# Where TensorE's operand tiles begin in SBUF: a fused attention and feed-forward kernel on one core

## The chip, the core and the metric

The kernel runs on one core of a Trainium2 chip. The metric is the device time of one execution in microseconds. The page and the trace are of one execution, taken by the hardware profiler.

## What is computed

For 4 batches, 8 heads, 576 positions and a head width of 64, two attentions are added: one over positions averaged by fours (each of its rows then stands for four positions), and one over a band of 7 positions. The sum, 2304 rows of 512, goes through two feed-forward layers.

```python
out_up = np.repeat(sm_attn(q_d, k_d, v_d), factor, axis=2)   # q_d: means of 4 positions
mask = np.abs(pos[:, None] - pos[None, :]) < factor          # factor = 4
out_local = softmax(where(mask, scale * q @ k.T, -1e9)) @ v
x = (out_up + out_local) as (2304, 512)
g = x @ w_gate                                               # 512 -> 1536
x = (g * sigmoid(g) * (x @ w_val)) @ w_out                   # 1536 -> 512
h = x @ w_in                                                 # 512 -> 2048
out = (h * clip(h + 3, 0, 6) / 6) @ w2_out                   # 2048 -> 512
```

## The kernel before, in words

Rows of x are worked on in five blocks of 512, 384, 512, 512 and 384 rows (`BLOCKS`, in units of 64). For each block a list of units is gone through: a unit is one 128-wide piece of a weight matrix. The kinds are G (gate), V (value), O (first output), H (second input) and P (second output). G and V of a block come first, with O two pieces behind, then H, with P two behind; this order of `units` and the look-ahead of `prefetch` set the order of nearly everything else. Attention for the next block is cut into small steps between the units (`down_main`, `chunk_scores`, `unit_values`, `step_x`).

Products are made in three parts of type float32r: each operand is kept as a high part, rounded by ScalarE, and a low part, the remainder, subtracted by VectorE. `split_unit` does it for a weight piece (`wr`, L230 and L231, out of the float32 weights `w32`, tag `wst`), `put_cols` for x (`xr`, L265 and L266), `run_unit` for the middle products (`g`, L965 and L966), `put_x2` for the first layer's result (`x2`, L1003 and L1004). TensorE then multiplies high by high, low by high and high by low.

`run_unit` has the two matmul lines. L948 serves G, V and H: the stationary operand is a 128 x 128 piece of `wr`, the moving one 512 or 384 columns of `xr` (G, V: the trace's pG, pV) or of `x2` (H: pH), into two PSUM banks in turn. L990 serves O and P: for O (aO) the stationary operand is `wr` and `g` moves; for P (aP) a 128 x 128 piece of `g` is stationary and 512 columns of `wr` move. Every such matmul has its own weight load.

Weights come from HBM once, as 8-byte words in block 0 (tag `w64`), are decoded on ScalarE and VectorE (`decode_a` L210, `decode_b` L219), and stored as float32 to `kept`, from which the later blocks load them (`load_unit` L178). The small constants are `half1` (0.5, a bias), `ones_last` (a mask of 28 numbers for either edge) and what those are made from (`ih`, `ind`). `softmax_d` keeps the negated maxima (`nm`) and the sums (`sd`) of the coarse attention. Before the first gate unit, matmuls on the bf16 tile `idle` fill TensorE (L94, L435).

SBUF tiles of a pool lie one behind the other, in the order in which their tags first appear, each on a multiple of 32 bytes of its partition. In the built program the tiles that matter begin at these bytes (modulo 256 in brackets), each further buffer of a tag one tile on:

| tile (tag) | bytes of one buffer | buffers | first byte |
|---|---|---|---|
| sl | 2048 | 3 | 21,536 (32) |
| x2 | 16,384 | 1 | 27,680 (32) |
| g | 4096 | 4 | 44,064 (32) |
| w64 | 4104, 4128 apart | 4 | 60,448 (32) |
| xr | 16,384 | 2 | 76,960 (160) |
| w32 (wst) | 4096 | 3 | 126,624 (160) |
| wr | 4096 | 4 | 138,912 (160) |

All slices of these that TensorE reads begin a multiple of 512 bytes into them, but for the first gate piece of block 0, which is done in 244 and 268 columns.

Of the kernel before, what the change touches and what calls it, by code (L numbers as in the profile page):

```python
# [10 lines left out]
F32 = mybir.dt.float32  # L11
# [3 lines left out]
I16 = mybir.dt.int16  # L15
# [6 lines left out]
P = 128  # L22
# [15 lines left out]
EXP_AT = 26  # L38

EARLY = 6  # L40


@with_exitstack
def tile_kernel(
# [14 lines left out]
    B, H, S, D = q.shape  # L59
    DM = H * D  # L60
# [4 lines left out]
    NJH = NJ // 2  # L65
    W = 7
# [3 lines left out]
    UT = 4 * NSEG  # L70
# [4 lines left out]
    UMAX = max(BLOCKS)  # L75
# [5 lines left out]
    cp = ctx.enter_context(tc.tile_pool(name="cp", bufs=1))  # L81
    sp = ctx.enter_context(tc.tile_pool(name="sp", bufs=2))
# [12 lines left out]

    ident = cp.tile([P, P], F32, name="ident")
    make_identity(nc, ident)
    half1 = cp.tile([P, 1], F32, name="half1")
    nc.gpsimd.memset(half1, 0.5)

    ones_last = []
    for side in range(2):
        ih = cp.tile([P, H], F32, tag=f"ih{side}", name=f"ih{side}")
        nc.gpsimd.memset(ih, 0.0)
        nc.gpsimd.affine_select(
            out=ih, in_=ih, compare_op=ALU.not_equal, fill=NEG,
            base=-(NSEG - 1) * side, pattern=[[-NSEG, H]], channel_multiplier=1,
        )
        ind = cp.tile([P, 1], F32, tag=f"ind{side}", name=f"ind{side}")
        nc.vector.tensor_reduce(ind, ih, axis=AX.X, op=ALU.add)  # L110
        on = cp.tile([P, 4, W], F32, tag=f"on{side}", name=f"on{side}")
        nc.gpsimd.memset(on, 0.0)
        sgn = 1 if side == 0 else -1
        nc.gpsimd.affine_select(
            out=on, in_=on, compare_op=ALU.is_ge, fill=1.0,
            base=-3 if side == 0 else 6, pattern=[[sgn, 4], [sgn, W]], channel_multiplier=0,
        )
        nc.vector.tensor_scalar(on, on, ind[:, 0:1], None, op0=ALU.mult)
        ones_last.append(on)
# [10 lines left out]
    def behind(ins):  # L130

        if front[0]:
            tc.keep_in_program_order(ins)
# [22 lines left out]
    raw = {}  # L156
# [3 lines left out]
    def view(t, i):  # L160
        return t[:, i % 2, :].rearrange("p (c e) -> p c e", c=NC)

    def load_raw(i):
        if units[i][2] == 0:
            load_unit(i)

    def load_kept(i):
        if units[i][2]:
            load_unit(i)

    def load_unit(i):
        kind, f, bi = units[i]
        if bi or not wide:
            if i % 2 == 0:
                w32[i // 2] = sp.tile([P, 2, DM], F32, tag="wst", name=f"w32_{i}", bufs=3)
        if bi:
            if i % 2 == 0:
                nc.sync.dma_start(w32[i // 2], kept[i % NU // 2])  # L178
            return
        src = wsrc[kind]  # L180
        if wide:
            src = src.bitcast(I16)
        m = 4 if wide else 1
        if kind in "GVH":
            src = src[:, f * P * m:(f + 1) * P * m].rearrange("(c p) f -> p c f", p=P)
        else:
            src = src[f * P:(f + 1) * P, :].rearrange("p (c e) -> p c e", c=NC)
        if wide:
            raw[i] = sp.tile([P, 4 * DM + 4], I16, tag="w64", name=f"w64_{i}", bufs=4)
            behind(nc.sync.dma_start(raw[i][:, 1:1 + 4 * DM].rearrange("p (c e) -> p c e", c=NC), src))  # L190
        else:
            nc.sync.dma_start(view(w32[i // 2], i), src)
# [500 lines left out]


    def softmax_d(pool, ps, nm_, bufs):
        nm = pool.tile([NJH, 2], F32, tag="nm", name=f"nm{nm_}", bufs=8)
        nc.vector.tensor_reduce(nm, ps, axis=AX.X, op=ALU.max, negate=True)
        pd = pool.tile([NJH, 2, NJ], F32, tag="pd", name=f"pd{nm_}", bufs=bufs)
        sd = pool.tile([NJH, 2], F32, tag="sd", name=f"sd{nm_}", bufs=8)
        for half in range(2):  # L700
            nc.scalar.activation(
                pd[:, half], ps[:, half], AF.Exp, bias=nm[:, half:half + 1], accum_out=sd[:, half:half + 1]
            )
        return pd, sd
# [155 lines left out]
    def down_main(b, dn, qk):  # L860
# [3 lines left out]
        def score(c):  # L864

            pss = []
            for par in range(2):
                ps = bank(("pa", "px")[par], f"pS{b}_{2 * c + par}")[:NJH, :2 * NJ]
                pss.append(ps.rearrange("p (g j) -> p g j", g=2))
            for half in range(2):  # L870
                for par in range(2):
                    rows = slice(par * D, par * D + D)
                    tc.keep_in_program_order(nc.tensor.matmul(  # L873
                        pss[par][:, half], qk["q"][rows, c, half * NJH:(half + 1) * NJH], qk["k"][rows, c, :],
                        start=True, stop=True,
                    ))

            def use():
                for par in range(2):
                    h = 2 * c + par  # L880
                    st[h] = softmax_d(ap, pss[par], f"{b}_{h}", 4)
                defer(1, lambda: [norm_d(*st[2 * c + par]) for par in range(2)])

            return use
# [154 lines left out]
    def load_ahead(n):  # L1039
        nonlocal loaded  # L1040
        while loaded < min(n, len(chunks)):
            load_chunk(*chunks[loaded])
            loaded += 1

    for bi in range(NB):
# [37 lines left out]
        for i in range(bi * NU, (bi + 1) * NU):  # L1083
# [21 lines left out]
            next(main, None)  # L1105
            if m == NU - EARLY:
                load_ahead(at + 1)
# [40 lines left out]
```

## Time and profile before

| | us |
|---|---|
| median of 3 runs (lowest, highest) | 1000.89 (1000.48, 1002.2) |
| span of the profiled execution | 998.5 |
| the median over this span | 2.4 |
| TensorE (PE) busy | 956.0 |
| VectorE (DVE) busy | 773.1 |
| ScalarE (ACT) busy | 529.7 |
| GpSimd (POOL) busy | 114.5 |

The span is the profiled execution's own time from its first to its last instruction; the runs' times hold what lies around it as well, so the profiled execution counts as 998.5 + 2.4 = 1000.9 us. Its mean granted TensorE clock was 0.978 of 2.4 GHz. A matmul's busy time in the groups overlaps with the next one's; the time from one matmul to the next is read from the chain or the timeline. PEld is the weight load, which runs beside PE.

### The profile page before, as it was taken

What the parts mean: (1) busy time and instruction counts of PE and PEld (TensorE: products, weight loads), DVE (VectorE), ACT (ScalarE), POOL (GpSimd) and SP (SyncE); (2) the same over time, 40 slices, a digit from 0 to 9 for tenths busy, and PEclk for the clock granted to TensorE, in tenths of its full rate; (3) what the DMA queues carried; (4) which work ended last, traced back from release to release, by engine and by line L of the source; (5) the groups of instructions that cost most, each with busy time, mean ns of one, the idle gap of its engine ahead of it and who ended that gap; (6) DMA issues with size and microseconds to landing.
All of it is one profiled execution on the core that took longest, in us unless ns stands there. A gap on an engine that the chain in (4) does not pass through costs nothing.

```text
span 998.5 us, 13508 instructions
## 1 busy us (share of the span) xinstructions
PE 956.0 (96%) x4797; PEld 797.6 (80%) x4800; DVE 773.1 (77%) x1237; ACT 529.7 (53%) x1115; POOL 114.5 (11%) x113
## 2 busy tenths in 40 slices
PE   8769999999998999996999999999999999999997
PEld 4558888777897987875888777788888888999996
DVE  6597986799989989996984699998346995545653
ACT  4566566876543577552334764453335444544553
POOL 5590000000046000004620000000000000000000
PEclk9769999999999999997999999999999999999999
DMA  9979899466789322356553122363322233533331
GB/s 191 201 197 344 292 331 324 144 217 231 250 244 289 117 85 87 118 177 205 159 172 106 58 70 96 104 228 121 102 88 89 83 104 109 154 125 124 125 126 52
DMA packets 83655, 160.72 MB, mean 161 GB/s; under 512 B 19460, under 2 KB 51716, under 8 KB 83588
## 3 DMA queue, kind: packets, MB, share of 16 engines
q1 hardware_dynamic: 78692, 142.03, 45.6%
q10 hardware_dynamic: 4896, 17.83, 5.1%
q8 instruction: 38, 0.62, 0.3%
q14 instruction: 29, 0.24, 0.1%
HBM read 137.29 MB, written 22.54 MB: 160 GB/s over the span
## 4 chain that ended last, share of the span: by engine, by line
PE 72%; issue 14%; DVE 4%; DMA 4%; POOL 3%; SPq 2%; ACT 0%; POOLq 0%; ACTq 0%; DVEq 0%
PE pH L948 16%; PE aP L990 16%; PE aO L990 13%; PE pG L948 13%; PE pV L948 12%; SPq L126 2%; DMA nq<-in_q_dram 1%; DVE wr L231 1%; POOL nq L290 1%; DMA w<-kept 1%; DMA vd<-in_v_dram 1%; PE pS L873 1%; PE pO L723 1%; DMA w<-in_moe_w_val_dram 1%; DMA nv<-in_v_dram 0%
## 5 line engine op out<-in xcount | busy, mean ns | idle before, releaser
L231 DVE TENSOR_TENSOR wr<-w,wr 128x512 fp32r<-128x512 f32 x340 | 238.3, 705 | 119.1 <-ACT wr L230 117.6
L230 ACT ACTIVATE wr<-w 128x512 fp32r<-128x512 f32 x340 | 212.0, 627 | 175.3 <-PE pV L948 53.9
L990 PE MATMUL aP<-wr,gH 128*128 128x512 f32 x864 | 216.3, 399 | 0.7 <-ACT wr L230 0.4
L948 PE MATMUL pH<-x,wr 128*128 128x512 f32 (+1 forms) x960 | 216.0, 376 | 0.0
L948 PEld LDWEIGHTS pH<-x,wr 128*128 128x128 f32 x960 | 173.6, 188 | 28.0 <-issue 2.7
L990 PEld LDWEIGHTS aP<-wr,gH 128*128 128x128 f32 x864 | 159.8, 188 | 39.0 <-issue 2.5
L948 PE MATMUL pG<-xr,wr 128*128 128x512 f32 (+3 forms) x732 | 161.3, 375 | 5.1 <-ACT xr L265 4.4
L948 PE MATMUL pV<-xr,wr 128*128 128x512 f32 (+1 forms) x720 | 156.1, 372 | 5.3 <-DVE wr L231 4.1
L990 PE MATMUL aO<-gV,wr 128*128 128x512 f32 (+1 forms) x720 | 156.3, 373 | 0.3 <-DVE wr L231 0.3
L948 PEld LDWEIGHTS pG<-xr,wr 128*128 128x128 f32 x732 | 136.2, 195 | 24.0 <-ACT xr L265 5.0
L948 PEld LDWEIGHTS pV<-xr,wr 128*128 128x128 f32 x720 | 132.7, 190 | 23.5 <-DVE wr L231 4.8
L990 PEld LDWEIGHTS aO<-gV,wr 128*128 128x128 f32 x720 | 131.6, 188 | 19.7 <-DVE wr L231 0.6
L963 ACT ACTIVATE h<-pH,half 128x512 f32<-128x512 f32 (+1 forms) x80 | 51.5, 644 | 71.4 <-PE pH L948 71.2
L954 ACT ACTIVATE sl<-pG 128x512 f32<-128x512 f32 (+1 forms) x60 | 33.2, 554 | 72.1 <-PE pG L948 70.5
L964 DVE SCALAR_TENSOR_TENSOR h<-h,pH 128x512 f32<-128x512 f32 (+1 forms) x80 | 50.5, 631 | 25.0 <-ACT h L963 24.2
L210 ACT ACTIVATE top<-w 128x512 f16<-128x512 bf16 x68 | 52.9, 790 | 15.6 <-DVE w L219 6.8
L782 DVE TENSOR_TENSOR pr<-q,k 128x1792 f32<-128x1792 f32 x27 | 57.0, 2113 | 3.9 <-DMA k<-in_k_dram 3.8
L290 POOL TENSOR_TENSOR nq<-nq 72x512 f32<-72x512 f32 x12 | 18.9, 1572 | 347.4 <-DMA nq<-in_q_dram 347.4
L965 ACT ACTIVATE gH<-h 128x512 fp32r<-128x512 f32 (+1 forms) x80 | 46.9, 587 | 19.1 <-DVE h L964 17.1
L966 DVE TENSOR_TENSOR gH<-h,gH 128x512 fp32r<-128x512 f32 (+1 forms) x80 | 50.6, 634 | 5.8 <-ACT gH L965 4.8
L819 DVE TENSOR_TENSOR pv<-sc,v 128x1792 f32<-128x1792 f32 x27 | 54.5, 2020 | 0.3
L965 ACT ACTIVATE gV<-sl 128x512 fp32r<-128x512 f32 (+1 forms) x60 | 35.2, 586 | 36.3 <-DVE sl L960 35.5
(127 smaller groups left out, 809.2 us busy)
## 6 DMA issues: line engine op xcount, KB each, us to landing
w<-kept SPq DMA_DIRECT2D x136, 512.0 KB
kept<-w ACTq DMA_DIRECT2D x34, 512.0 KB
w<-in_moe_w_out_dram SPq DMA_DIRECT2D x28, 512.0 KB
w<-in_moe_w_in_dram SPq DMA_DIRECT2D x16, 512.0 KB
w<-in_moe_w_gate_dram SPq DMA_DIRECT2D x12, 512.0 KB
w<-in_moe_w_val_dram SPq DMA_DIRECT2D x12, 512.0 KB
out_dram<-os SPq DMA_DIRECT2D x16, 256.0 KB
nq<-in_q_dram SPq DMA_DIRECT2D x12, 288.0 KB
```

Of the source, the lines that this page charges most:

```text
L210: behind(nc.scalar.activation(halves(top[i % 2], 2, F16)[:, :, 1], h3.bitcast(BF16), AF.Copy))
L230: behind(nc.scalar.activation(r[:, 0], s, AF.Copy))
L231: behind(nc.vector.tensor_tensor(r[:, 1], s, r[:, 0].bitcast(F32), op=ALU.subtract))
L782: nc.vector.tensor_tensor(pr, qt[:, a:a + SUB, None, :].to_broadcast([P, SUB, W, D]), win(kt, a, SUB), op=ALU.mult)
L819: nc.vector.tensor_tensor(pr, pe[:, a:a + SUB, :, None].to_broadcast([P, SUB, W, D]), win(vt, a, SUB), op=ALU.mult)
L948: nc.tensor.matmul(ps[:, cs], r[:, a, c], x[:, c, b_, cs], start=part is HIGH and a == c == 0, stop=part is LOW and c == NC - 1,)
L954: nc.scalar.activation(sl, ps, AF.Silu)
L963: nc.scalar.activation(h, ps, AF.Relu, scale=1 / 6, bias=half1[:, 0:1])
L964: nc.vector.scalar_tensor_tensor(h, h, 1.0, ps, op0=ALU.min, op1=ALU.mult)
L965: nc.scalar.activation(g[:, 0, :nt], h, AF.Copy)
L966: nc.vector.tensor_tensor(g[:, 1, :nt], h, g[:, 0, :nt].bitcast(F32), op=ALU.subtract)
L990: nc.tensor.matmul(ps, **one, start=f_ == 0 and a == b_ == 0, stop=f_ == nf - 1 and b_ == 1,)
```

## The change

The small constants (`half1` and the two masks) share one tile of 384 bytes, `consts`; `ih` and `ind` become slices of a buffer of the tag `sl`; `nm` and `sd` share one tile; and `w64` is 4160 bytes instead of 4104. The tiles behind them move by at most 96 bytes:

| tile (tag) | first byte before (modulo 256) | after |
|---|---|---|
| sl | 21,536 (32) | 21,504 (0) |
| x2 | 27,680 (32) | 27,648 (0) |
| g | 44,064 (32) | 44,032 (0) |
| w64 | 60,448 (32) | 60,416 (0), further buffers at 64, 128, 192 |
| xr | 76,960 (160) | 77,056 (0) |
| w32 (wst) | 126,624 (160) | 126,720 (0) |
| wr | 138,912 (160) | 139,008 (0) |

The buffers of each but `w64` all have the remainder of the first. Every engine's instructions and its waits on semaphores stand in the same order in both built programs, SyncE's DMAs too; only names and addresses differ. The changed kernel's lines lie 2 to 4 lines lower in the file.

```diff
@@ -38,6 +38,8 @@
 EXP_AT = 26
 
 EARLY = 6
+
+SMALL = 384
 
 
 @with_exitstack
@@ -95,20 +97,22 @@
 
     ident = cp.tile([P, P], F32, name="ident")
     make_identity(nc, ident)
-    half1 = cp.tile([P, 1], F32, name="half1")
+    consts = cp.tile([P, SMALL // 4], F32, name="consts")
+    half1 = consts[:, 56:57]
     nc.gpsimd.memset(half1, 0.5)
 
     ones_last = []
     for side in range(2):
-        ih = cp.tile([P, H], F32, tag=f"ih{side}", name=f"ih{side}")
+        tmp = sp.tile([P, UMAX * UT], F32, tag="sl", name=f"tmp{side}", bufs=3)
+        ih = tmp[:, :H]
         nc.gpsimd.memset(ih, 0.0)
         nc.gpsimd.affine_select(
             out=ih, in_=ih, compare_op=ALU.not_equal, fill=NEG,
             base=-(NSEG - 1) * side, pattern=[[-NSEG, H]], channel_multiplier=1,
         )
-        ind = cp.tile([P, 1], F32, tag=f"ind{side}", name=f"ind{side}")
+        ind = tmp[:, H:H + 1]
         nc.vector.tensor_reduce(ind, ih, axis=AX.X, op=ALU.add)
-        on = cp.tile([P, 4, W], F32, tag=f"on{side}", name=f"on{side}")
+        on = consts[:, 28 * side:28 * side + 28].rearrange("p (t w) -> p t w", w=W)
         nc.gpsimd.memset(on, 0.0)
         sgn = 1 if side == 0 else -1
         nc.gpsimd.affine_select(
@@ -186,7 +190,7 @@
         else:
             src = src[f * P:(f + 1) * P, :].rearrange("p (c e) -> p c e", c=NC)
         if wide:
-            raw[i] = sp.tile([P, 4 * DM + 4], I16, tag="w64", name=f"w64_{i}", bufs=4)
+            raw[i] = sp.tile([P, 4 * DM + 32], I16, tag="w64", name=f"w64_{i}", bufs=4)
             behind(nc.sync.dma_start(raw[i][:, 1:1 + 4 * DM].rearrange("p (c e) -> p c e", c=NC), src))
         else:
             nc.sync.dma_start(view(w32[i // 2], i), src)
@@ -693,10 +697,10 @@
 
 
     def softmax_d(pool, ps, nm_, bufs):
-        nm = pool.tile([NJH, 2], F32, tag="nm", name=f"nm{nm_}", bufs=8)
+        ns = pool.tile([NJH, 2, 2], F32, tag="ns", name=f"ns{nm_}", bufs=8)
+        nm, sd = ns[:, 0], ns[:, 1]
         nc.vector.tensor_reduce(nm, ps, axis=AX.X, op=ALU.max, negate=True)
         pd = pool.tile([NJH, 2, NJ], F32, tag="pd", name=f"pd{nm_}", bufs=bufs)
-        sd = pool.tile([NJH, 2], F32, tag="sd", name=f"sd{nm_}", bufs=8)
         for half in range(2):
             nc.scalar.activation(
                 pd[:, half], ps[:, half], AF.Exp, bias=nm[:, half:half + 1], accum_out=sd[:, half:half + 1]
```

## Rows read from the trace of the kernel before

**Rows 1.** The page: busy us of each engine, share of the span, instructions.

```profile
PE 956.0 (96%) x4797; PEld 797.6 (80%) x4800; DVE 773.1 (77%) x1237; ACT 529.7 (53%) x1115; POOL 114.5 (11%) x113
```

**Rows 2.** Windows by stage: stretch and its length, busy of each engine, clock, DMA share.

```profile
75.00:168.00 93.00, 93.00 (x413) 76.35 (x413) 77.35 (x107) 59.46 (x97) 0.00 (x0) 0.99 0.94 327
168.00:275.00 107.00, 106.69 (x517) 82.67 (x516) 96.09 (x175) 77.22 (x167) 0.00 (x0) 1.00 0.63 215
275.00:335.00 60.00, 54.46 (x298) 52.87 (x297) 55.18 (x61) 24.57 (x45) 30.76 (x24) 0.97 0.77 233
335.00:400.00 65.00, 63.44 (x378) 54.62 (x377) 59.19 (x125) 46.25 (x121) 0.00 (x0) 1.00 0.31 100
400.00:467.00 67.00, 58.20 (x285) 48.61 (x285) 62.57 (x98) 31.88 (x60) 8.39 (x6) 0.97 0.48 149
...
553.00:656.00 103.00, 102.91 (x496) 78.68 (x495) 92.06 (x177) 59.40 (x140) 0.00 (x0) 1.00 0.28 93
656.00:756.00 100.00, 100.00 (x438) 81.95 (x437) 64.13 (x78) 39.94 (x67) 0.00 (x0) 1.00 0.38 127
```

**Rows 3.** Waits of PE: total us, times, longest.

```profile
PE pqT L303 <- POOL dnq L291: 8.1, 2, 5.4
...
PE pV L948 <- DVE wr L231: 4.1, 2, 3.5
```

**Rows 4.** Groups of PE by shape: form xcount | busy us, mean ns.

```profile
L990 PE MATMUL aP<-wr,gH 128*128 128x512 f32 x864 | 216.3, 399 | 0.7 <-ACT wr L230 0.4 <-DVE wr L231 0.3
L948 PE MATMUL pH<-x,wr 128*128 128x512 f32 x576 | 143.8, 399 | 0.0
L990 PE MATMUL aO<-gV,wr 128*128 128x512 f32 x432 | 103.3, 395 | 0.0
L948 PE MATMUL pG<-xr,wr 128*128 128x512 f32 x420 | 102.2, 399 | 0.4 <-ACT xr L265 0.4
L948 PE MATMUL pV<-xr,wr 128*128 128x512 f32 x432 | 101.4, 390 | 0.0
L948 PE MATMUL pH<-x,wr 128*128 128x384 f32 x384 | 72.3, 340 | 0.0
L948 PE MATMUL pV<-xr,wr 128*128 128x384 f32 x288 | 54.8, 344 | 5.3 <-DVE wr L231 4.1 <-ACT sl L954 1.1
L990 PE MATMUL aO<-gV,wr 128*128 128x384 f32 x288 | 53.0, 339 | 0.3 <-DVE wr L231 0.3
L948 PE MATMUL pG<-xr,wr 128*128 128x384 f32 x288 | 52.0, 335 | 0.0
```

**Rows 5.** The chain that ended last: start us, us to the next piece, work.

```profile
709.00 5.44 PE pV L948 x24
714.45 5.59 PE aO L990 x24
...
798.57 5.59 PE pH L948 x24
804.16 5.57 PE aP L990 x24
...
853.67 4.16 PE pV L948 x24
...
866.15 4.22 PE aO L990 x24
...
937.41 4.22 PE pH L948 x24
```

**Rows 6.** Timeline of PE, bf16 filler matmuls: start us, us, instruction.

```profile
6.21 0.59 PE L435 MATMUL fTq<-idle 128*128 128x512 bf16 x2
6.64 0.25 PE L446 MATMUL fTq<-ident,fnq 96*128 96x96 f32 x1
```

**Rows 7.** Groups by shape, of DVE: form xcount | busy us, mean ns | idle before.

```profile
L231 DVE TENSOR_TENSOR wr<-w,wr 128x512 fp32r<-128x512 f32 x340 | 238.3, 705 | 119.1 <-ACT wr L230 117.6
...
L966 DVE TENSOR_TENSOR gH<-h,gH 128x512 fp32r<-128x512 f32 x48 | 32.9, 686 | 4.1 <-ACT gH L965 3.3
```

## The prediction

> **What bounds the kernel now.** I read the page's first part first, then the stretches by stage, then what PE waits for, then the counts of matmuls by shape, and last the chain of work that ended last, which gives the time from one matmul to the next. TensorE (PE) is busy 956.0 us of the 998.5 us span, 96% [rows 1]. By stages it is full: in the gate/value/out stage of block 0 (75 to 168 us) 93.00 of 93.00 us, in 656 to 756 us 100.00 of 100.00, and in the H/P stages, where VectorE (DVE) works hardest, still 106.69 of 107.00 and 102.91 of 103.00 [rows 2]. Only 275 to 467 us is different: PE 54.46 of 60, 63.44 of 65 and 58.20 of 67 us, DVE 55.18, 59.19 and 62.57 [rows 2], and there lie the largest waits that PE has: 8.1 us for GpSimd's sums of q, 4.1 us for split weights from DVE [rows 3]. So the time is, outside of that stretch, the count of matmuls times the time from one to the next. The mean duration in the group rows (about 400 ns) is no measure of it, since matmuls overlap; the chain is, for its pieces follow each other without a gap (709.00 + 5.44 = 714.44, where the next begins).
>
> The chain shows what this change can touch. 24 matmuls of 512 columns take 5.44 us for pV, 5.59 for aO, 5.59 for pH, 5.57 for aP; 24 of 384 columns take 4.16 for pV, 4.22 for aO and pH [rows 5]. That is 226.7 ns against some 232.5 at 512 columns, and 173.3 against 175.8 at 384. pV and pH come from the same line, the same loops, the same two PSUM banks and the same weight buffers. What is different between them is the moving tile: xr lies at 160 modulo 256, x2 at 32, and wr, the stationary one, at 160. aO moves g (32) against wr (160); aP moves wr (160) against g (32). So the pair with the same remainder takes less time, and the three pairs that are 128 bytes apart take more. The clock is not the difference: from 656 to 756 us, where the 5.44 and the 5.59 stand side by side, it is granted at 1.00 [rows 2], the level of 2.4 GHz.
>
> A second thing stands in the trace: the bf16 fillers, also 512 columns with a weight load each, start 215 ns apart (two of them from 6.21 to 6.64 us) [rows 6]. 512 columns at 2.4 GHz are 213.3 ns. So even the better float32r pair pays 13.3 ns per matmul over the columns, at 384 columns too (173.3 - 160.0), and the fillers pay under 2. The fillers' tile lies at 32 modulo 256 as well, so the same offset does not hurt an operand of half the bytes.
>
> **The change part by part.** Every engine has the same instructions with the same waits in the same order; no DMA is added or moved. So there are no new waits by construction, and each term is a duration that may change.
>
> *The small tiles.* Constants, ih/ind and the softmax statistics move into shared tiles. Their instructions and waits are the same, so I cost them at nothing; the one-time ones run in the first microseconds beside the filler matmuls. If that were wrong it would show as a later first gate matmul, not in the stages.
>
> *The operand tiles.* All four, moving and stationary, now begin at 0 modulo 256, so every big matmul has a pair with the same remainder, as pG and pV have now. The price of that pair is 5.44 and 4.16 us for 24. Matmuls with unequal remainders at 512 columns: aP 864, pH 576, aO 432, together 1872 [rows 4], 78 groups of 24. With 5.58 as the middle of the three rows, 78 x (5.58 - 5.44) = 10.9 us. At 384 columns: pH 384 and aO 288, 28 groups, 28 x (4.22 - 4.16) = 1.7 us. Together 12.6 us of PE time. pG and pV keep theirs.
>
> Not all of it reaches the end. 168 to 467 us holds the H/P stage of block 0 (192 pH and 192 aP, 16 groups, 2.2 us) and block 1 (6 groups of aO and 8 of pH at 0.06, 6 of aP at 0.14, 1.7 us): 3.9 us. There DVE is busy 96.09 + 55.18 + 59.19 + 62.57 = 273.0 of 299 us, 91% [rows 2], and PE waits for it and for GpSimd behind loads. What is late next when PE is earlier is the split of the weights on DVE. I let half of the 3.9 be lost, 2.0 us; the ends are 0 and 3.9. Sum: 12.6 - 2.0 = 10.6 us.
>
> *The price at 0 that no row shows.* The better pair of today begins 32 bytes behind a multiple of 64 and of 128; no float32r operand here begins at 0. The low end is the fillers' 215 ns: for 384 columns, 215 - 128/2.4 = 161.7. In groups of 24 that is 5.16 and 3.88. It would give 78 x 0.42 = 32.8, for pG and pV (852 at 512, 35.5 groups) 35.5 x 0.28 = 9.9, 28 x 0.34 = 9.5 and for their 576 at 384 columns 24 x 0.28 = 6.7: 58.9 us. The high end is that the pairs at 0 take the 5.58 us of today's unequal pairs. I take the 226.7 in between, because it is the only row of a float32r pair with equal remainders.
>
> *sl and the float32 weights.* They are read and written by ScalarE, DVE and DMAs, not by PE. DVE's split at remainder 160 takes 705 ns, its subtraction on g at 32 takes 686 on the same shape [rows 7]. Whatever 0 gives, between those it is 340 x 19 ns = 6.5 us of DVE time spread over the span, behind PE; I cost it at nothing. It would count only in 275 to 467 us.
>
> **A rule against the row.** The Trainium skill, TensorE: Matmul & The Clock Gate, "Step-by-step: what each phase is for", says that PE has two independent read ports, so that loading the next weights takes no read bandwidth from the running matmul. And SBUF - State Buffer, in its specifications, gives lines of 16 bytes, on which 32 and 160 both begin. By these two the offsets would decide nothing and the saving would be 0. The trace does not agree as far as it goes: 226.7 against 232.5 ns with the same code. But they stand for the rival that follows second.
>
> **The rivals.**
>
> (1) *The offset itself was the cost of all of them* (chance 0.25). If the 13.3 ns over the columns come from beginning 32 bytes into a wider unit of reading, then 0 takes them away for pG and pV too. For it: 226.7/213.3 and 173.3/160.0 are the same 32 columns on top, a whole number, and the fillers don't pay. Against it: the fillers begin at 32 too, and the 13.3 ns may be what a float32r weight load costs a running matmul wherever it lies. It would give 58.9 us of PE time. Half of 17.3 us in 168 to 467 us would be lost to DVE, some 3 us in 553 to 656 us (DVE 92.06 of 103 [rows 2]), and 1 to 2 us in 75 to 168 us, where the DMAs are at 0.94. That leaves 46 us, and 955 us.
>
> (2) *Addresses modulo 256 are not what makes pH take longer than pV* (0.11). x2 and g lie below 60 KB, xr above 76 KB, so a place in the memory would explain the rows as well, and no tile changes its place by more than 96 bytes. Then PE stays as it is, and the time is 1001 us.
>
> (3) *Equal zeros collide* (0.14). Two read streams that both begin at 0 may meet in the same part of the memory at each start, and pG and pV lose what they have at 160/160 while the others gain nothing. Price: 35.5 groups x 0.14 + 24 x 0.06 = 5.0 + 1.4 = 6.4 us, 1007 us. It decides as soon as a group of 24 pV of 512 columns takes over 5.44 + 10.9/35.5 = 5.75 us with the others gaining in full, or over 5.44 at all with the others unchanged. For it: an equal remainder is not proven to be the reason. Against: the only equal pair of the trace takes the least time.
>
> **How the numbers follow.** The forecast, equal remainders at today's price of the equal pair, has 0.50. Against the profiled execution: 998.5 - 10.6 = 987.9 us of span. The runs' median, 1000.89, is 2.4 us over this span, so I add 2.4: 990.3, given as 990. Its own range, with the stretch on DVE losing nothing or all and the groups at 5.57 or 5.59, is 987 to 993. What a measurement here can tell from no change is about 0.2%, 2 us. Faster is the forecast and (1), less a little for the case that DVE and the waits take back more: 0.74. Within 0.2% is (2) and that little: 0.12. Slower is (3): 0.14. The range leaves out (3) and the lower part of (1), where nothing is lost to DVE (942 us): 950 to 1002.
>
> **What would show it.** Right: in the chain of the changed kernel, 24 pH, aO and aP of 512 columns take 5.44 us like pV, and 4.16 at 384; DVE's share grows in 168 to 467 us, and the wait for GpSimd's sums stays about 8 us, since its loads queue behind the stores of block 1, which come earlier too. For (1), pV itself falls towards 5.16. For (2), pV and pH stay 0.14 us apart. For (3), pV rises to 5.58. A first gate matmul that starts much later than before, or DVE operations on sl, w or wr that change by over 20 ns, would make the sum wrong from another side.

## The result, and the profile after

The changed kernel takes 993.45 us in the median (988.92 to 994.62, 4 runs), the kernel before 1001.55 beside it; the ratio is 0.9913, 95% interval 0.9884 to 0.9942. A second set of runs (e10) gave 0.9897 (0.9878 to 0.9916). The forecast was 990; 8.1 to 9.3 us came of the 10.6 that were expected. The profiled execution has a span of 992.8 us, 5.7 less than before. That is less than the medians differ by. In every run whose span is known the time is 1.7 to 1.9 us longer than the span, so the profiled execution of before counts as some 1000.3 us, not as the median's 1000.9. It is 1.2 below its median here, and that of the change, 994.62 us, is 1.2 above its own.

The page of the changed kernel, first part: busy us, share of the span, instructions, to be held against [rows 1].

```profile
PE 949.6 (96%) x4800; PEld 797.0 (80%) x4800; DVE 775.1 (78%) x1237; ACT 529.0 (53%) x1115; POOL 113.6 (11%) x113
```

PE is as full as before and has 6.4 us less to do. Where, the groups by shape tell (form, count, busy us, mean ns, idle before), beside [rows 4]:

```profile
L994 PE MATMUL aP<-wr,gH 128*128 128x512 f32 x864 | 213.0, 395 | 0.8 <-ACT wr L234 0.4 <-DVE wr L235 0.3
L952 PE MATMUL pH<-x,wr 128*128 128x512 f32 x576 | 141.4, 395 | 0.0
L952 PE MATMUL pV<-xr,wr 128*128 128x512 f32 x432 | 101.1, 390 | 0.0
L994 PE MATMUL aO<-gV,wr 128*128 128x512 f32 x432 | 100.7, 390 | 0.0
L952 PE MATMUL pH<-x,wr 128*128 128x384 f32 x384 | 71.6, 338 | 0.0
L994 PE MATMUL aO<-gV,wr 128*128 128x384 f32 x288 | 52.6, 336 | 1.7 <-DVE wr L235 1.7
```

aP fell by 3.3 us, pH by 2.4 and 0.7, aO by 2.6 and 0.4, together 9.4; pV at 512 columns, which had equal remainders already, by 0.3. The chain that ended last (start us, us to the next piece) shows it per 24 matmuls, beside [rows 5]:

```profile
706.63 5.44 PE pV L952 x24
712.07 5.44 PE aO L994 x24
...
795.07 5.49 PE pH L952 x24
800.55 5.44 PE aP L994 x24
...
857.36 4.16 PE pV L952 x24
861.52 4.16 PE aO L994 x24
...
932.20 4.18 PE pH L952 x24
936.38 4.12 PE aP L994 x18
```

aO and aP have pV's time to the hundredth, 5.44 for 5.59 and 5.57; pH has 5.49. At 384 columns aO has 4.16 and pH 4.18. That is what the forecast named as its sign, but for the last hundredths of pH; pV did not move, which is against rivals (1) and (3).

The waits of PE (total us, times, longest), beside [rows 3]:

```profile
PE pqT L307 <- POOL dnq L295: 7.5, 2, 5.4
...
PE pV L952 <- DVE wr L235: 5.5, 2, 4.6
```

The wait for GpSimd's sums stays (8.1 to 7.5 us), the waits for DVE's split weights grow by some 2.8 us (pV's from 4.1 to 5.5, aO's at 384 columns from 0.3 to 1.7, as its row above has it).

### The profile page after: what moved, and what is told of

The parts are those of the page before. It is cut to its first block, busy times and chain, and to the rows that moved or that the text cites. A ratio compares the mean times of both kernels' runs of the same rounds, so it can differ in the third digit from the quotient of the medians.

```text
span 992.8 us, 13511 instructions
## 1 busy us (share of the span) xinstructions
PE 949.6 (96%) x4800; PEld 797.0 (80%) x4800; DVE 775.1 (78%) x1237; ACT 529.0 (53%) x1115; POOL 113.6 (11%) x113
## 4 chain that ended last, share of the span: by engine, by line
PE 67%; issue 15%; DVE 11%; DMA 3%; ACT 2%; POOL 1%; SPq 0%; ACTq 0%; POOLq 0%; DVEq 0%
PE pH L952 14%; PE aP L994 13%; PE aO L994 12%; PE pG L952 12%; PE pV L952 12%; DVE wr L235 2%; DMA nq<-in_q_dram 1%; DMA w<-kept 1%; DVE pv L823 1%; ACT held L565 1%; DVE gH L970 1%; POOL nq L294 1%; PE pS L877 1%; DVE xf L852 1%; DMA w<-in_moe_w_val_dram 1%
## 5 line engine op out<-in xcount | busy, mean ns | idle before, releaser
L235 DVE TENSOR_TENSOR wr<-w,wr 128x512 fp32r<-128x512 f32 x340 | 240.8, 713 | 113.2 <-ACT wr L234 111.8
L994 PE MATMUL aP<-wr,gH 128*128 128x512 f32 x864 | 213.0, 395 | 0.8 <-ACT wr L234 0.4
L952 PE MATMUL pH<-x,wr 128*128 128x512 f32 (+1 forms) x960 | 213.0, 372 | 0.0
L994 PE MATMUL aO<-gV,wr 128*128 128x512 f32 (+1 forms) x720 | 153.3, 368 | 1.7 <-DVE wr L235 1.7
L967 ACT ACTIVATE h<-pH,consts 128x512 f32<-128x512 f32 (+1 forms) x80 | 51.5, 644 | 68.5 <-PE pH L952 68.5
```

Source lines behind the costliest of these rows:

```text
L235: behind(nc.vector.tensor_tensor(r[:, 1], s, r[:, 0].bitcast(F32), op=ALU.subtract))
L952: nc.tensor.matmul(ps[:, cs], r[:, a, c], x[:, c, b_, cs], start=part is HIGH and a == c == 0, stop=part is LOW and c == NC - 1,)
L967: nc.scalar.activation(h, ps, AF.Relu, scale=1 / 6, bias=half1[:, 0:1])
L994: nc.tensor.matmul(ps, **one, start=f_ == 0 and a == b_ == 0, stop=f_ == nf - 1 and b_ == 1,)
```

## The experiments

Three theories stood after the result. **A**: what counts is the distance of the two operands' addresses modulo 256, that is, the difference of their remainders. **B**: each operand has to begin at 0 of some unit (64, 128 or 256 bytes). **C**: the place in the memory counts, not the remainder.

**The shared small tiles alone** (e2). Padding puts the operands back where they lay.

```diff
-SMALL = 384
+SMALL = 416
...
-            raw[i] = sp.tile([P, 4 * DM + 32], I16, tag="w64", name=f"w64_{i}", bufs=4)
+            raw[i] = sp.tile([P, 4 * DM + 4], I16, tag="w64", name=f"w64_{i}", bufs=4)
```

> The small constants and statistics share tiles as in the change, but the padding is such that sl, x2, g, xr, w32 and wr lie where they lay before (32 and 160 modulo 256). Theories A and B: as before, ratio 1.000 within 0.003, 24 pH of 512 columns 5.58 us. If the sharing itself were what gained: ratio 0.991, like the change.

Ratio 1.0003 (0.9985 to 1.0021), and the chain has the times of before:

```profile
713.58 5.59 PE aO L994 x24
```

The sharing of tiles gains nothing by itself.

**Equal, but at 160** (e3).

```diff
-SMALL = 384
+SMALL = 544
```

> The changed kernel with 160 bytes more ahead of sl, so that sl, x2, g, xr, w32 and wr all lie at 160 modulo 256: equal, but not 0. Theory A: as the change, ratio 0.991 within 0.003, 24 matmuls of 512 columns 5.44 us for pH, aO and aP. Theory B: not better than before, ratio 1.00 or more, 5.58 us or more.

Ratio 0.9912 (0.9892 to 0.9932), as the change. Its chain:

```profile
709.20 5.44 PE aO L994 x24
...
792.18 5.49 PE pH L952 x24
797.67 5.44 PE aP L994 x24
```

Theory B falls: all operands are at 160, which is a multiple of none of its units, and the times are those of the change, pH's 5.49 too.

**Each operand on a multiple of 128, but 128 apart** (e4): x2 and g at 128, xr and wr at 0. Each buffer of w64 is 32 bytes shorter, so that nothing behind w64 moves.

```diff
-            raw[i] = sp.tile([P, 4 * DM + 32], I16, tag="w64", name=f"w64_{i}", bufs=4)
+            raw[i] = sp.tile([P, 4 * DM + 16], I16, tag="w64", name=f"w64_{i}", bufs=4)
...
+            sp.tile([P, 32], F32, tag="pad", name="pad", bufs=1)
             held = sp.tile([P, NC, 2, UMAX * UT], F32R, tag="x2", name="held", bufs=1).bitcast(F32)
```

> The changed kernel with 128 bytes ahead of x2: x2 and g lie at 128, xr, w32 and wr at 0 modulo 256. The distance of before is restored, each operand on a multiple of 128. Theory A: as before, ratio 1.000 within 0.003, pH, aO and aP 5.58 us for 24, pV 5.44. Theory B with a unit of 64 or 128 bytes: as the change, 0.991. Theory B with 256 bytes: as theory A here, but then the kernel with all at 160 has to be slower.

The chain has the times of before back:

```profile
709.06 5.44 PE pV L953 x24
714.50 5.59 PE aO L995 x24
...
769.87 5.60 PE aP L995 x24
...
866.14 4.23 PE aO L995 x24
```

The whole time is 999.24 us, ratio 0.9971 (0.9954 to 0.9987): not the 0.991 of the change, but some 3 us less than before, with the same matmul times. Where these come from isn't known: the profiled execution, with a span of 998.6 us against 998.5, does not show them. Against the all-at-160 kernel of the same set (993.38 us), making the pairs unequal costs 5.9 us.

**Every pair 128 apart** (e8): wr alone is moved, so pG and pV lose their equal remainders too.

```diff
+        if not i:
+            sp.tile([P, 128 // 4], F32, tag="pad4", name="pad4", bufs=1)
         r = sp.tile([P, 2, NC, P], F32R, tag="wr", name=f"wr{i}", bufs=4)
```

> The changed kernel with 128 bytes ahead of wr, so that wr lies at 128 and xr, x2, g at 0 modulo 256: every pair of operands is 128 apart, pG's and pV's too. Theory A: 24 matmuls of 512 columns take 5.58 us in all five kinds, 24 of 384 columns 4.22; against the change 12.6 us more PE time for pH, aO and aP and 6.4 for pG and pV, so slower than before by some 3 to 8 us, ratio 1.003 to 1.008. If a place in the memory or an operand's own offset from 128 decided: 5.44 throughout, ratio 0.991.

Ratio 1.0033 (1.0014 to 1.0051), and the two kinds that had never been touched now pay as well:

```profile
710.37 5.60 PE pV L954 x24
715.97 5.60 PE aO L996 x24
721.57 5.60 PE pG L954 x24
...
855.91 4.23 PE pV L954 x24
```

xr lies here where it lies in the changed kernel, wr 128 bytes on. So theory C falls: the same tile in the same place is at 5.44 or 5.60 us by the other operand's remainder.

**A scan of offsets** (e1, e5). Behind the last P unit, groups of 30 matmuls read a slice of the last g (stationary) and of the last wr (moving). Each slice begins some bytes into its tile, and both tiles lie at 0 modulo 256. A group is named by the two offsets, so 64/0 has the moving operand 64 bytes ahead. The code is that of the second scan, without the calls.

```diff
+    def scan(name, mov, st, cols=512, wide=P, half=False):
+        ps = bank("mm", name, 2)
+        for n in range(30):
+            lhs, rhs = gs[:, st // 4:st // 4 + wide], rm[:, mov // 4:mov // 4 + cols]
+            if half:
+                lhs = gs.bitcast(BF16)[:, st // 2:st // 2 + wide]
+                rhs = rm.bitcast(BF16)[:, mov // 2:mov // 2 + cols]
+            tc.keep_in_program_order(
+                nc.tensor.matmul(ps[:wide, :cols], lhs, rhs, start=n == 0, stop=n == 29)
+            )
```

The first scan opened a bank anew with each matmul.

> The changed kernel with 900 more matmuls behind its last P unit (30 each of 30 pairs of offsets, results unused), so its time is longer by about 200 us and says nothing; the time from one matmul to the next in each group of 30 is read. Theory A (only the distance of the two operands modulo 256 counts): 226.7 ns at equal offsets (0/0, 16/16, 32/32, 128/128, 160/160), about 232.5 ns at a distance of 128, something between or above at the other distances, the same for either sign. Theory B (each operand has to begin at 0 modulo 64, 128 or 256): 226.7 ns at 0/0 and more at 32/32 and 160/160. Theory C (a place in the memory counts): the same time in every group, since the tiles are the same. Stationary tiles of 64 and 32 columns: if the 13.3 ns over the columns are taken by the weight load, about 220 and 217 ns; if they belong to the moving operand, 226.7 still. bf16 at any offset: 215 ns.

It gave no answer on float32r: in nearly every group the matmuls alternated between some 320 and 240 ns, 0/0 included, and that hides the offsets. Its bf16 groups could be read: 216 ns with both operands at 32, with both at 0, and at 0/128:

```profile
1203.49 6.65 PE L1137 MATMUL mov32st32xbf<-wr,gH 128*128 128x512 bf16 x30
1209.98 6.64 PE L1137 MATMUL mov0st0xbf<-wr,gH 128*128 128x512 bf16 x30
1216.46 6.64 PE L1137 MATMUL mov0st128xbf<-wr,gH 128*128 128x512 bf16 x30
```

The second scan keeps a group in one bank.

> The scan again, now each group of 30 into one PSUM bank as one accumulation (in the first scan the two banks in turn made every second matmul wait, 320 and 240 ns). Results unused; the whole time says nothing. Theory A: after some matmuls 226.7 ns at equal offsets (0/0, 4/4, 16/16, 32/32, 64/64, 128/128, 160/160) and at 0/256, about 232.5 at a distance of 128, and more than 226.7 at the other distances. Theory B: more than 226.7 at 4/4, 16/16 or 32/32. A distance below 226.7 ns would be a better layout than the change's. Stationary tiles of 64 and 32 columns: about 220 and 217 ns if the 13.3 ns over the columns are due to the weight load, 226.7 if they are the moving operand's own. 384 columns: 173.3 at 0/0, 176 at 0/128.

Its timeline, at a granted clock of 1.00 (start us, us, instruction; a group's time is the next one's start less its own):

```profile
979.82 6.97 PE L1137 MATMUL mov0st0x<-wr,gH 128*128 128x512 f32 x30
986.62 7.13 PE L1137 MATMUL mov0st4x<-wr,gH 128*128 128x512 f32 x30
993.60 6.97 PE L1137 MATMUL mov0st16x<-wr,gH 128*128 128x512 f32 x30
1000.40 7.15 PE L1137 MATMUL mov0st32x<-wr,gH 128*128 128x512 f32 x30
...
1028.40 7.16 PE L1137 MATMUL mov0st128x<-wr,gH 128*128 128x512 f32 x30
1035.41 7.17 PE L1137 MATMUL mov0st160x<-wr,gH 128*128 128x512 f32 x30
...
1063.11 6.96 PE L1137 MATMUL mov0st256x<-wr,gH 128*128 128x512 f32 x30
1069.91 7.26 PE L1137 MATMUL mov4st0x<-wr,gH 128*128 128x512 f32 x30
...
1090.93 7.04 PE L1137 MATMUL mov64st0x<-wr,gH 128*128 128x512 f32 x30
1097.81 7.17 PE L1137 MATMUL mov96st0x<-wr,gH 128*128 128x512 f32 x30
...
1132.85 7.29 PE L1137 MATMUL mov4st4x<-wr,gH 128*128 128x512 f32 x30
1139.98 7.07 PE L1137 MATMUL mov16st16x<-wr,gH 128*128 128x512 f32 x30
1146.88 7.01 PE L1137 MATMUL mov32st32x<-wr,gH 128*128 128x512 f32 x30
1153.73 6.99 PE L1137 MATMUL mov64st64x<-wr,gH 128*128 128x512 f32 x30
```

| offsets, moving/stationary | ns of one (mean of 30) |
|---|---|
| 0/0, 0/16, 0/256 | 226.7 |
| 0/240 | 227.3 |
| 32/32, 64/64, 128/128, 160/160 | 227.3 to 228.3 |
| 64/0, 0/192 | 229.3 |
| 0/32, 0/48, 0/64, 0/96, 0/128, 0/160, 0/224 | 233.0 to 234.0 |
| 32/0, 96/0, 128/0, 160/0, 192/0, 224/0 | 232.7 to 234.3 |
| 16/16, 16/0 | 230.0, 231.3 |
| 0/4 | 232.7 |
| 4/0, 4/4 | 236.7, 237.7 |

So for starts on multiples of 32, which is all that the kernel has, theory A holds in its main part: 226.7 ns at the distance 0 and 256, about 233 at nearly all others. It doesn't in that both signs were to cost the same: 229.3 where the moving operand is 64 bytes ahead (64/0, 0/192), 233 where it is 64 behind (0/64, 192/0). For starts off 32 it doesn't hold: 4/4 and 16/16 are not at 226.7, while the stationary operand may begin 16 bytes on at no cost (0/16), or 16 bytes short of 256 at next to none (0/240). No pair that was tried is below 226.7. Two more things: the groups at 32/32 to 160/160 don't begin at 226.7. In 32/32 the first ten matmuls take 225 to 236 ns and the rest 226.7, which is why their means are above it. And a stationary operand of 64 columns is not quicker: that group, at 0/0, begins at 1174.23 us and the next at 1181.15, 230.7 ns each, neither of the two values expected.

**Two other distances in the kernel** (e6, e7): as e4, with pads ahead of x2, g and xr of 64, 32 and 32 bytes (e6: x2 at 64, g at 96) or 32, 32 and 64 (e7: x2 at 32, g at 64).

> The changed kernel with x2 at 64 and g at 96 modulo 256; xr, w32 and wr stay at 0. Theory A: pG and pV as in the change (5.44 us for 24 of 512 columns); pH (distance 64) and aO, aP (96) between 5.44 and 5.7, whatever the distance costs, each the same in every block. If only a distance of 128 costs something: all at 5.44 and the time as the change's, 990 to 995 us. If every distance but 0 costs: 5.58 for the three, 997 to 1004 us.

> The changed kernel with x2 at 32 and g at 64 modulo 256; xr, w32 and wr stay at 0. Theory A: pG and pV 5.44 us for 24; pH now at the distance 32, aO and aP at 64. aO here and pH in the kernel with x2 at 64 must agree, as the same distance. If every distance but 0 costs: about 5.58 for the three and 997 to 1004 us.

One run each: 1001.36 and 1000.12 us. In e7 aO, whose moving operand is 64 ahead, takes 5.51 us for 24, and aP, where it is 64 behind, 5.60:

```profile
715.03 5.51 PE aO L997 x24
...
770.10 5.60 PE aP L997 x24
```

The scan says 229.3 x 24 = 5.50 and 233 x 24 = 5.59 for these: the matmuls in the kernel follow it, sign included. In e6, at distance 96, aO and aP take 5.61; its pH, at 64 ahead like aO in e7, takes 5.50 to 5.52. At 384 columns the distances 64 and 32 cost nothing there: 24 pH take 4.16 us in both kernels.

**Columns, and reading the same again** (e9). The scan's groups with fewer columns, and three in which the moving operand is 128, 32 or 8 columns read again and again.

> Groups of 30 accumulating matmuls behind the last P unit as before, now over the number of columns, both operands at 0 and the stationary at 128; and three groups that read the same 128, 32 or 8 columns again and again. Results unused. What the equal pair still pays over its columns at 2.4 GHz is 13.3 ns at 512 and at 384. If it is one cost per matmul: 13.3 ns at every count, 280.0/240/.. by columns/2.4 + 13.3. If the moving operand is read in units of 32 columns and one unit more than it holds: steps of 13.3 ns, the same time for 512, 504 and 496 columns. If it comes from reading ever new bytes: the groups that read 8 or 32 columns again are at 215 ns as bf16 is; otherwise at 226.7.

The groups of 496, 480 and 464 columns start at 996.60, 1003.30 and 1009.80 us: 496 columns take 223.3 ns and 480 take 216.7, 16.7 over columns/2.4 both times. 320 columns pay 13.3, 288 pay 11.7. So it is neither one cost per matmul nor a staircase of 32 columns. The last groups, of 512 columns:

```profile
1084.69 6.97 PE L1136 MATMUL again128x<-wr,gH 128*128 128x512 f32 x30
1091.50 7.26 PE L1136 MATMUL again32x<-wr,gH 128*128 128x512 f32 x30
1098.60 6.70 PE L1136 MATMUL again8x<-wr,gH 128*128 128x512 f32 x30
```

Reading 8 columns again takes 6.70 us for the 30 where 128 take 6.97 and 32 take 7.26. So what is paid over the columns is no constant, and neither expectation came true, 226.7 ns throughout or bf16's 215. It changes with the bytes that the moving operand reads, or with the repeating way of reading them; the two weren't told apart. What it is, stays open.

**The change once more** (e10), unedited.

> The changed kernel itself once more, beside the kernel before on this chip, to narrow the interval and to have a second profile. Theory A and the first result: ratio 0.991 within 0.002; 24 aO, pG and pV 5.44 us; pH and aP somewhat above where small matmuls come between.

992.52 us (5 runs), ratio 0.9897 (0.9878 to 0.9916). Its chain has 5.44 us for 24 aO, pG and pV, 5.47 to 5.49 for pH and 5.44 to 5.47 for aP, as expected.

## Why the prediction was right, and where it was off

**The mechanism was right.** Equal remainders give every kind pV's time in an unbroken run, whatever the remainder is (e3), unequal ones take it away (e4), from pV too (e8). Why the chip has it so, no run shows. The price of 5.44 us, taken from the only equal pair of [rows 5], was measured for aO and aP. The place in the memory, rival (2), fell with e8; a cost of the offset itself, rival (1), with pV's unchanged 5.44 us and with 0/0 and 0/256 at the same 226.7 ns as the steady part of 32/32; the collision of equal zeros, rival (3), is the opposite of what was found.

**The term that was mis-sized** is the 78 x 0.14 of the matmuls at 512 columns. For aO it held: 2.6 us by the groups against 18 x 0.15 = 2.7. For pH and aP at 512, 60 groups and 8.4 us were forecast, and 2.4 + 3.3 = 5.7 came. What was left out is that their stages are broken up by the attention's small matmuls, and that behind such a break an equal pair does not run at 226.7 ns at once. Pieces of 12 aP or pH, in the chain of before:

```profile
604.07 2.83 PE aP L990 x12
606.90 2.80 PE pH L948 x12
610.35 3.00 PE pH L948 x12
```

and of the changed kernel:

```profile
602.35 2.83 PE aP L994 x12
605.18 2.72 PE pH L952 x12
608.55 3.00 PE pH L952 x12
```

The first and the third follow small matmuls and gained nothing. The second follows the first without a break and gained in full.

The starts of single matmuls show why. Of the 24 aP that follow small matmuls at 611.52 us in the change, the first is 312 ns ahead of the next, six more take 228 to 236 ns, and only then come 226 to 227; before, the same aP stay at 228 to 241 behind their first. A change from 384 to 512 columns does the same without a small matmul: aP at 927.92 us begins with nine matmuls of 224 to 236 ns, and 18 aP take 4.12 us there for 18 x 226.7 = 4.08. A change of the remainder can do it too, as in the second scan's 32/32. Among the matmuls that are followed by another within 300 ns, the mean time to the next fell for aP from 232.6 to 228.5 ns and for pH at 512 from 232.7 to 228.3; for aO, which is hardly broken up, it fell from 232.9 to 226.9.

So the H/P stage of block 2 (556.40 to 659.69 us before, 555.08 to 657.67 after) became 0.70 us shorter for a forecast of 2.2, the one of block 3, with few breaks (758.61 to 849.50, 755.59 to 844.85), 1.63 of 2.2.

**The half of 3.9 us that was to be lost** before 467 us can't be settled to a microsecond. The H/P stage of block 0, from its first pH to the first pG of block 1, takes 100.5 us in the traces of the change, e3 and e10, and 101.3 in those of before, e2 and e4: 0.8 of the 2.2, for the reason just given. Behind it the waits and the clock decide. The profiled execution was 0.37 us ahead at the first pH of block 0 (173.11 for 173.48), 0.94 at the piece of pH that starts at 248.06 us (249.00 before), and 0.88 behind at the 12 pG that start at 468.24 (467.36): in this trace nothing of the 3.9 was left by then.

At the pV behind these it was 0.26 ahead (472.31 for 472.57), but by the clock: after the wait for GpSimd's sums the 12 pG ran at a granted clock of 0.50 (the level of 1.2 GHz) and took 5.21 us before; in the change the clock was back at 1.00 by 471.3 us, and they took 4.07. At 0.50 the pair does not matter: the kernel with all pairs 128 apart (e8) and the kernel before, whose pG has an equal pair, both take 427 ns for a pG there. The waits for DVE grew as shown, but in e2, with the matmul times of before, PE waited in block 1 for DVE's wr by 5.3 us (before pV) too. So they vary by as much from one execution to the next. From 472 us on the lead grows to 5.75 us at the last aP (983.67 to 977.92), with 0.7 us of waits in the way.

**That the time came so near is in part luck.** From the first pH of block 2 to the start of the last aP matmul, 7.1 of the 12.6 us were forecast (16 x 0.14 twice, 6 x 0.15, 14 x 0.06 and 6 x 0.14). The traces of before, e2 and e4 take 435.3 to 435.4 us for it, those of the change, e3 and e10 take 430.7 to 430.9: 4.6 us. The spans of these three and three differ by 6.2 us in the mean, and the times of e4 and e3 by 5.9. By these, the equal pairs are worth about 6 us. The other 2 to 3 of the 8.1 to 9.3 us are as open as the 3 us that e4 gained with unequal pairs. The forecast's own range, 987 to 993, has both medians at its upper end.

**The small tiles** cost nothing, as said (e2). The sign that was named for them, a later first gate matmul, did appear: 59.65 us in the change and 59.36 in e10, for 57.68 before. But e2 and e3, with the same shared tiles, have it at 55.67 and 55.63, and by the first pH the change is ahead, as said.

**sl and the float32 weights**: DVE's split takes 713 ns with w32 and wr at 0 (the change, e10) and 705 with both at 160 ([rows 7], e3), outside of the 686 to 705 that were expected: 340 x 8 ns = 2.7 us of DVE time. What this adds to the waits of block 1 was not separated; the whole time is the same without it (e3).

The rule of the Trainium skill (TensorE: Matmul & The Clock Gate, "Step-by-step: what each phase is for"), that loading the next weights takes no read bandwidth from the running matmul, agrees with the bf16 groups, 216 ns at a distance of 128 as at 0. For float32r the time depends on where the stationary operand begins, 226.7 against 233 ns, so the saving of 0 that the prediction worked out as a rival did not come, and the measurement decides. Whether the weight load is what the matmul meets, no run shows.

## What to carry to other kernels

When two loops with the same code and the same shapes have different times per matmul in the chain at the same granted clock, compare where their operands begin. For float32r at the granted 2.4 GHz, put the stationary and the moving tiles at the same remainder modulo 256: here the sizes of two tiles, `consts` and `w64`, set it. Expect the gain in long unbroken runs of matmuls; in the first 7 to 10 matmuls behind a small matmul or a change of columns it mostly doesn't come.

## What the runs showed that was not expected

- The time of a float32r matmul depends on the pair of addresses, with a period of 256 bytes: 226.7 ns at 0/0 and 0/256, 233.7 at 0/128, and not alike for both signs: 229.3 at 64/0, 233.0 at 0/64.
- Behind a small matmul, a change of columns or of the remainder, an equal pair can take some 7 to 10 matmuls (224 to 236 ns) before it is at 226.7. It isn't always so: in the second scan 0/0, behind aP of the same remainder, and 0/16, behind 0/4, were there from their first.
- At the granted clock of 0.50 (1.2 GHz) equal and unequal pairs took the same 427 ns.
- A narrower stationary operand did not shorten the matmul: 230.7 ns at 64 columns, 231.7 at 32, against 226.7 at 128.
- Starts off a multiple of 16 bytes can cost most: 236.7 ns at 4/0, 237.7 at 4/4, but 232.7 at 0/4.
